# A prelude of attention and weight products: key sums by matmul, queries' shift on ScalarE, and a denser schedule

## The chip, the core and the metric

The kernel runs on one NeuronCore of a Trainium2 chip. The metric is the device time of one execution in microseconds, as the median of the runs shown. TensorE does matmuls and transposes, VectorE and ScalarE read its results out of PSUM, GpSimd works on SBUF, and DMA queues are fed by SyncE, ScalarE and GpSimd.

## The reference

Three layers follow one another over 2304 tokens (4 batches of 576). The kernel computes all of it in fp32 accuracy.

```python
def phi(x):                                   # per head, 64 -> 128 -> 256 features
    proj = x @ w_phi
    proj = proj - np.max(np.abs(proj), axis=-1, keepdims=True)
    return np.concatenate([np.exp(proj), np.exp(-proj)], axis=-1)
q_p, k_p = phi(q), phi(k)
kv = einsum('bhsf,bhsd->bhfd', k_p, v)
z  = sum(k_p, axis=2)                         # the key sums
attn = (q_p @ kv) / (q_p @ z + 1e-6)
x = ((attn @ w1) * (attn @ w2)) @ w3 @ w_out  # moe1
# moe2: route each token to one of 8 experts, relu(x @ ew1[e]) @ ew2[e], times the gate
```

## The kernel before

**Stages.** A first stage, the prelude, does two things at once. It folds `w3 @ w_out` into one matrix W (`build_w`, L216) and splits w1 and w2 into a high and a low fp32r part (`load_w12`, L199), and it works on attention for the first batch. Then moe1 runs over nine blocks of 256 tokens, each of eight `ab_unit`s (L596) and four products with W, with the rest of attention strewn between; then come the expert slots of moe2.

**W's units.** The weights come as 64-bit numbers, and `f64_to_f32` (L124) makes fp32 of each 512 KB tile by three integer operations on VectorE (L132, L134, L136); there are 8 tiles of w_out, 16 of w3 and 16 of w1 and w2. `wo_a` and `wo_b` (L235 on) convert and transpose w_out's chunks and multiply them with the expert embeddings, over a bank `pl` that four `wo_b` share. A `w_unit` (L275) is eight native fp32 matmuls, 16 records in the trace; there are 16 such units, two for each of eight column chunks, and each second one ends in splits of two banks `pw` into `wph` (ScalarE) and `wpl` (VectorE, L112).

**Attention's units.** The features of one head are two exponentials of a projection shifted by its largest magnitude. For keys, `phi_tile` (L307) projects a tile of 128 tokens and four heads into a PSUM bank `pphi`, VectorE takes the largest magnitude `mx` (L325), and `key_feats` makes eight activations on ScalarE (L339, L340). Then `kv` (L448) multiplies the features with v (`kv_native`, L394) into one bank that all pieces of a batch share. For z the features of all pieces are first added up on VectorE in `kacc` (L461), and `sums` (L468) multiplies the total with a block of ones, 32 columns wide, once for each of four heads (`key_sums`, L397). `fin` transposes both and splits them. For queries, `query_p` (L344) subtracts the largest magnitude from the projection on VectorE (L347) into `pt`; `tr` transposes one head of it (L539), and two activations (L542, L543) make the features `F`, which are split into `Hh` and `Ll`; `num` multiplies them with kv and z (bank `po`), and for each second head VectorE divides (`den`, L564, and `xf`, L568) and the result is split into moe1's input.

While `native` is set, projections are single fp32 matmuls (four records a tile) and the input tiles `qkraw` and `v` are requested from ScalarE's queue (`queue`, L367). Afterwards, the tile is split into `qkh` (ScalarE) and `qkl` (VectorE or GpSimd), the projection takes six fp32r matmuls, and requests go through SyncE's queue.

**What sets the order.** TensorE's instructions run in the order in which the program writes them (`manual_schedule(engines={PE})`, L1082 and L1106). The order on the other engines is made by the framework's scheduler when the kernel is built, and then fixed. Every unit of attention has a time in a planner's units: a key piece takes `KEY_T` 1.9, a head's query 1.04 + 0.65 times a quarter of its tiles; projections are put `LEAD_Q` 3.5 (queries) or `LEAD_K` 2.25 (keys) ahead, numerators `LEAD_N` 2.95 behind their transposes. `due[blk]` (L1072) is the time at which block blk of moe1 has its input; `due[0]` stands 1.5 behind the last numerator of the first chunk of 256 tokens. `attend(until)` (L1076) writes out all units whose time is below `until`. W's units cost 0.5 (`wo_a`, `wo_b` and the like, 18 of them) or 3.1 (`w_unit`, 16), 58.6 in total, and after each one the loop calls

```python
attend(START_T * (done / tot) ** START_P)     # START_T 32.0, START_P 0.7
```

so that at W's end all attention due before 32.0 is written. Then `native` is cleared, buffers for moe1 are made, `fill_scratch` writes fills to DRAM through SyncE's queue, and `attend(due[0])` writes what is left before moe1's first block.

**PSUM.** Three banks (`pm`) serve W, moe1 and routing, five (`pa`) all of attention, and in the prelude also `wo_a`, `wo_b` and `wo_c`.

Of the kernel before, what the change touches and what calls it, by code (L numbers as in the profile page):

```python
# [9 lines left out]
F32 = mybir.dt.float32  # L10
# [4 lines left out]
AF = mybir.ActivationFunctionType  # L15
# [8 lines left out]
NF = 128  # L24
# [3 lines left out]
P = 128  # L28
# [22 lines left out]
LEAD_Q = 3.5  # L51
LEAD_N = 2.95
GAP_K = 2.0
START_T = 32.0
START_P = 0.7
RAW64 = 3
PTB = 5
# [37 lines left out]
class Kern:  # L95
# [248 lines left out]
    def query_p(self, p3, m, keep):  # L344

        pt = self.ap.tile([P, 4, NF], F32, tag="ptk" if keep else "pt", name="pt", bufs=2 if keep else PTB)
        self.nc.vector.tensor_tensor(out=pt, in0=p3,  # L347
                                     in1=m.rearrange("p (h o) -> p h o", o=1).to_broadcast([P, 4, NF]),
                                     op=ALU.subtract)
        return pt  # L350
# [36 lines left out]
    def kv_native(self, kvp, v, kfs, r0, r1, first, last):  # L387
# [4 lines left out]
        for r in range(2):  # L392
            for c in range(2):
                self.nc.tensor.matmul(out(kvp, c * D, D, r * 256), lhsT=v[r0:r1, (2 * r + c) * D:(2 * r + c + 1) * D],  # L394
                                      rhs=kfs[r][r0:r1, :, c * NF:(c + 1) * NF],
                                      start=first and r == 0, stop=last and r == 1)
    def key_sums(self, zp, acc):  # L397

        for h in range(4):
            self.nc.tensor.matmul(zp[32 * h:32 * h + 32, 0:256].rearrange("p (s f) -> p s f", s=2), lhsT=self.one32,  # L400
                                  rhs=acc[h // 2][:, :, (h % 2) * NF:(h % 2 + 1) * NF], start=True, stop=True)

    def kv_split(self, b, pair, pv, pz):

# [14 lines left out]
    def key_units(self, out, time, b):  # L419

        nc = self.nc
        pieces = self.pieces(b)
        whole = int(pieces[0][1] > 0)
        for g in range(2):
            kvp = [None, None]
            acc = []
            for n, (t, r0, r1) in enumerate(pieces):
                st = {}

                def phi(st=st, t=t, n=n, g=g, r0=r0, r1=r1, whole=whole):  # L430
                    self.ph = int(b > 0)
                    st["v"] = self.load_v(t, g)
                    if r0:

                        st["f"] = self.kept[g]
                        return
                    keep = r1 < P

                    kind = ("kfk", 4) if keep else ("kacc", KACC) if n == whole else ("kf", KB_)
                    st["f"] = self.key_feats(*self.phi_tile("k", t, g), kind)  # L440
                    if keep:
                        self.kept[g] = st["f"]

                if not r0:
                    phi.raw = ("k", t, g)
                out.append((time - LEAD_K, phi))

                def kv(st=st, n=n, r0=r0, r1=r1, kvp=kvp, g=g, acc=acc):  # L448
                    if n == 0:
                        kvp[0] = self.app.tile([P, 512], F32, tag="pa", name="kv")  # L450
                    self.ph = int(b > 0)
                    last = n == len(pieces) - 1
                    self.kv_native(kvp[0], st["v"], st["f"], r0, r1, n == 0, last)
                    todo = [(st["f"], r0, r1)]
                    if n == whole:

                        todo = [(self.kept[g], *pieces[0][1:])] if whole else []
                        acc[:] = st["f"]
                    for f, a, e in todo if n >= whole else ():
                        for r in range(2):  # L460
                            nc.vector.tensor_tensor(out=acc[r][a:e], in0=acc[r][a:e], in1=f[r][a:e], op=ALU.add)  # L461
                    if last:

                        x = self.ap.tile([P, 512], F32, tag="pt", name="kvs0", bufs=PTB)
                        nc.scalar.copy(x, kvp[0])
                        kvp[0] = x

                def sums(kvp=kvp, acc=acc):  # L468
                    kz = self.app.tile([P, 512], F32, tag="pa", name="kz")
                    self.key_sums(kz, acc)  # L470
                    x = self.ap.tile([P, 320], F32, tag="xf", name="kvs1", bufs=1)
                    nc.scalar.copy(x[:, :256], kz[:, :256])
                    kvp[1] = x

                out.append((time + KV_D / 2, kv))
                time += KEY_T - 0.65 * (r0 > 0)

            def fin(kvp=kvp, g=g):
                self.ph = int(b > 0)
                ps = [self.app.tile([P, 512], F32, tag="pa", name=x) for x in ("pkv", "pkz")]  # L480
                for x, p, w in zip(kvp, ps, (512, 256)):
                    for a in range(0, w, P):
                        nc.tensor.transpose(p[:, a:a + P], x[:, a:a + P], self.ident)
                for r in range(2):
                    self.kv_split(b, 2 * g + r, *ps)

            out.append((time + SUM_K, sums))
            out.append((time + FIN_K, fin))
        return time + GAP_K
# [543 lines left out]
def tile_kernel(ctx, tc, qT, kT, vv, w_phi, w1, w2, w3t, w_out, emb, tau, ew1, ew2, out):  # L1033
    k = Kern(tc)
    nc = tc.nc
    maxrow = (NE - 1) * CAP + NT

    def pool(stack, name, side="left", **kw):
        return stack.enter_context(tc.tile_pool(name=name, bufs=kw.pop("bufs", 1), side=side, reuse_waits="tile", **kw))

    def regs(e, row, engines):
        return (nc.values_load(e, engines=engines, min_val=0, max_val=NE - 1),
                nc.values_load(row, engines=engines, min_val=0, max_val=maxrow))
# [28 lines left out]
    due = [ready[min(i for i, e in enumerate(chunk_end) if e >= (blk + 1) * BLK)] for blk in range(NBLK)]  # L1072
# [3 lines left out]
    def attend(until):  # L1076
        nonlocal ai
        while ai < len(attn) and attn[ai][0] < until:
            attn[ai][1]()
            ai += 1  # L1080

    with ExitStack() as c0, tc.manual_schedule(engines={PE}):  # L1082
        sp = pool(c0, "start")
        k.attn_init(apool, papool, sp, qT, kT, vv)
        k.attn_loads([u for _, u in attn])
        k.constants(cp, sp, w_phi)
        k.more_constants(cp, sp, pm, emb, tau)
        attend(START_0)
        lw = k.load_w12(sp, w1, w2, wt)
        wu = k.build_w(sp, pm, papool, w3t, w_out, wph, wpl)  # L1090

        tot = sum(c for c, _ in wu)
        done, n = 0.0, len(lw)
        for c, u in wu:
            u()
            done += c
            while lw and n - len(lw) < n * done / tot:
                lw.pop(0)()
            attend(START_T * (done / tot) ** START_P)
        k.native = False  # L1100
    mp = pool(c1, "moe1")
    for i in (1, 2):
# [2 lines left out]
    with ExitStack() as order:  # L1105
        order.enter_context(tc.manual_schedule(engines={PE}))  # L1106
        late = None
        for blk in range(NBLK):
            units, route, tail = k.moe1_units(blk, mp, pm, wt, wph, wpl, x2d, tab)
            attend(due[blk])  # L1110
            for i, (c, u) in enumerate(units):
                if i == 3 and late:
                    late()
                    late = None
                    if blk == EARLY:
# [5 lines left out]
                        e, row = regs(*k.early_slot(wa, pm), {SP})  # L1121
# [6 lines left out]
                n = (blk - EARLY) * len(units) + i - 3  # L1128
# [7 lines left out]
                else:  # L1136
                    b0 = EARLY - TAILB
                    f = ((blk - b0) * len(units) + i + 1) / (TAILB * len(units) + 3)
# [5 lines left out]
    with tc.manual_schedule(engines={ENG[x] for x in MENG}):  # L1144
# [6 lines left out]
        for s in range(NSTAT + 1):  # L1151
            loads = splits = ()
            for i, u in enumerate(cur[1] + cur[2]):
# [10 lines left out]
                if s < NSTAT and go:  # L1164
                    e, row = regs(k.ri[0:1, s:s + 1], k.ri[0:1, 4 + s:5 + s], {SP})
# [18 lines left out]
                if s == NSTAT and i == 2:  # L1184

                    cnt = nc.values_load(k.ri[0:1, 8:9], min_val=0, max_val=NLOOP)
                    e, row = regs(k.ri[0:1, 16:17], k.ri[0:1, 32:33], {SP})
# [7 lines left out]
    with tc.tile_pool(name="rest", bufs=1) as rp:  # L1195
        with tc.For_i(1, cnt, 1) as i:
            e, row = regs(k.ri[0:1, ds(i + 16, 1)], k.ri[0:1, ds(i + 32, 1)], {SP})
# [41 lines left out]
```

## Time and profile before

| | us |
|---|---|
| median of 3 runs | 867.17 (865.34 to 867.81) |
| the profiled execution's own time | 866.59 |
| its span, first to last instruction | 864.9 |
| TensorE busy in the span | 819.2 (95%) |
| VectorE | 536.9 (62%) |
| ScalarE | 402.9 (47%) |
| GpSimd | 240.4 (28%) |

The profile is of one execution. PE is TensorE's matmuls (PEld its weight loads), DVE VectorE, ACT ScalarE, POOL GpSimd, SP SyncE; a name with q is the engine's queue. A busy share is an average over stages with different limits, so the views below are asked for stretches of the span. A wait is the idle time of an engine just before an instruction, put down to what released it. One fp32 matmul is two records in the trace.

### The profile page before, as it was taken

What the parts mean: (1) busy time and instruction counts of PE and PEld (TensorE: products, weight loads), DVE (VectorE), ACT (ScalarE), POOL (GpSimd) and SP (SyncE); (2) the same over time, 40 slices, a digit from 0 to 9 for tenths busy, and PEclk for the clock granted to TensorE, in tenths of its full rate; (3) what the DMA queues carried; (4) which work ended last, traced back from release to release, by engine and by line L of the source; (5) the groups of instructions that cost most, each with busy time, mean ns of one, the idle gap of its engine ahead of it and who ended that gap; (6) DMA issues with size and microseconds to landing.
All of it is one profiled execution on the core that took longest, in us unless ns stands there. A gap on an engine that the chain in (4) does not pass through costs nothing. (4 is left out here: it accounts for less than half of the span.)

```text
span 864.9 us, 15449 instructions
## 1 busy us (share of the span) xinstructions
PE 819.2 (95%) x5730; PEld 734.5 (85%) x5730; DVE 536.9 (62%) x1226; ACT 402.9 (47%) x1105; POOL 240.4 (28%) x257
## 2 busy tenths in 40 slices
PE   6789978999999999999999999989999999999996
PEld 4467767998899987999888999989998898989974
DVE  6889996656779866797757794644375452432200
ACT  5454445455676557674555752213334342433211
POOL 2112353431255312463212642130013301211010
PEclk9999998899999999999999999989999999999998
DMA  6666642001211011210021000032207441622410
GB/s 205 223 202 201 198 125 76 26 22 60 57 24 50 13 56 52 55 45 19 26 67 44 25 14 1 26 105 80 91 26 248 161 147 43 194 87 86 158 41 15
DMA packets 63535, 73.43 MB, mean 85 GB/s; under 512 B 7832, under 2 KB 50072, under 8 KB 63458
## 3 DMA queue, kind: packets, MB, share of 16 engines
q1 hardware_dynamic: 53010, 58.88, 21.8%
q0 software_dynamic: 3680, 9.72, 3.3%
q10 hardware_dynamic: 6768, 3.82, 1.5%
q8 instruction: 46, 0.75, 0.4%
q14 instruction: 31, 0.25, 0.1%
HBM read 61.71 MB, written 10.95 MB: 84 GB/s over the span
## 5 line engine op out<-in xcount | busy, mean ns | idle before, releaser
L112 POOL TENSOR_TENSOR Ll<-F,Hh 128x512 fp32r<-128x512 f32 (+1 forms) x64 | 93.6, 1463 | 104.0 <-ACT Hh L104 95.7
L120 PE MATMUL px<-wph,abh 128*128 128x260 f32 x288 | 84.1, 292 | 4.9 <-DVE ab L609 3.5
L120 PE MATMUL pab<-xh,w1h 128*128 128x256 f32 x288 | 84.4, 293 | 0.1
L122 PE MATMUL px<-wph,abl 128*128 128x260 f32 x288 | 82.6, 287 | 0.0
L121 PE MATMUL px<-wpl,abh 128*128 128x260 f32 x288 | 82.5, 286 | 0.0
L121 PE MATMUL pab<-xl,w1h 128*128 128x256 f32 x288 | 81.8, 284 | 0.0
L122 PE MATMUL pab<-xh,w1l 128*128 128x256 f32 x288 | 81.8, 284 | 0.0
L120 PE MATMUL pab<-xh,w2h 128*128 128x256 f32 x288 | 81.5, 283 | 0.0
L121 PE MATMUL pab<-xl,w2h 128*128 128x256 f32 x288 | 81.5, 283 | 0.0
L122 PE MATMUL pab<-xh,w2l 128*128 128x256 f32 x288 | 81.4, 283 | 0.0
L120 PE MATMUL ph<-xsh,wth 128*128 128x256 f32 (+1 forms) x256 | 75.9, 296 | 0.6 <-ACT xsh L104 0.6
L121 PE MATMUL ph<-xsl,wth 128*128 128x256 f32 (+1 forms) x256 | 75.7, 296 | 0.5 <-DVE xsl L112 0.5
L122 PE MATMUL ph<-xsh,wtl 128*128 128x256 f32 (+1 forms) x256 | 75.6, 295 | 0.0
L285 PE MATMUL pw<-wo,y 128*128 128x260 f32 x256 | 64.6, 408 | 5.0 <-DVE wpl L112 3.3
L112 POOL TENSOR_TENSOR qkl<-qkraw,qkh 128x256 fp32r<-128x256 f32 x52 | 38.6, 745 | 110.5 <-ACT qkh L104 107.7
L607 ACT COPY a<-pab 128x256 f32<-128x256 f32 x72 | 27.2, 378 | 86.9 <-PE pab L122 71.2
L564 DVE RECIPROCAL den<-den 128x256 f32<-128x256 f32 (+1 forms) x32 | 62.3, 1947 | 7.8 <-ACT den L559 7.7
L943 DVE SCALAR_TENSOR_TENSOR hh<-ph,hh 128x256 fp32r<-128x256 f32 (+1 forms) x96 | 31.1, 353 | 57.9 <-ACT hh L939 51.0
L609 DVE TENSOR_TENSOR ab<-pab,a 128x256 f32<-128x256 f32 x72 | 30.4, 423 | 55.8 <-ACT a L607 55.4
L285 PEld LDWEIGHTS pw<-wo,y 128*128 128x128 f32 x256 | 50.8, 203 | 15.1 <-DVE wpl L112 4.9
L120 PEld LDWEIGHTS px<-wph,abh 128*128 128x128 f32 x288 | 55.6, 193 | 8.6 <-DVE ab L609 3.7
L325 DVE TENSOR_REDUCE mx<-pphi 128x4 f32<-128x512 f32 x72 | 49.2, 686 | 18.4 <-PE pphi L122 8.8
(230 smaller groups left out, 2408.9 us busy)
## 6 DMA issues: line engine op xcount, KB each, us to landing
wraw<-in_moe_w_dram SPq DMA_DIRECT2D x32, 512.0 KB
raw<-in_moe_w_dram SPq DMA_DIRECT2D x16, 512.0 KB
raw<-in_moe_w3t_dram SPq DMA_DIRECT2D x16, 512.0 KB
x2d<-x SPq DMA_DIRECT2D x18, 256.0 KB
raw<-in_moe_w_out_dram SPq DMA_DIRECT2D x8, 512.0 KB
pw<-in_moe_w_dram SPq DMA_DIRECT2D x8, 512.0 KB
v<-in_v_dram SPq DMA_DIRECT2D x30, 128.0 KB
qkraw<-in_qT_dram SPq DMA_DIRECT2D x27, 128.0 KB
```

The costliest lines, as they stand in the source:

```text
L112: e.tensor_tensor(out=out, in0=a, in1=b, op=ALU.subtract)
L120: nc.tensor.matmul(out, lhsT=lh, rhs=rh, start=start, stop=False)
L121: nc.tensor.matmul(out, lhsT=lh, rhs=rl, start=False, stop=False)
L122: nc.tensor.matmul(out, lhsT=ll, rhs=rh, start=False, stop=stop)
L285: nc.tensor.matmul(pss[u][:, :HB], lhsT=y[:, j, :], rhs=wo[:, jc, u, :], start=jc == 0, stop=jc == 7)
L325: nc.vector.tensor_reduce(out=m, in_=p3, axis=AX.X, op=ALU.max, apply_absolute_value=True)
L564: nc.vector.reciprocal(den[:, :n], den[:, :n])
L607: nc.scalar.copy(a, ps[:, :BLK])
L609: nc.vector.tensor_tensor(out=ab, in0=ps[:, BLK:], in1=a, op=ALU.mult)
L943: nc.vector.scalar_tensor_tensor(out=lo(h, i, j), in0=x, scalar=0.0, in1=h[:, i:j].bitcast(F32), op0=ALU.max, op1=ALU.subtract)
```

## The change

The key sums of the first batch are made by TensorE from each piece's features, accumulated in a bank of their own that is held from the first piece to the last; the additions on VectorE stay for the other batches only. While `native` is set, the queries' shift is made by a negation and four activations with a bias on ScalarE in place of one subtraction on VectorE. `START_T` goes: the attention written during W now runs up to `due[0]`, and reaches it at 1/1.04 of W's cost.

```diff
     def query_p(self, p3, m, keep):
         pt = self.ap.tile([P, 4, NF], F32, tag="ptk" if keep else "pt", name="pt", bufs=2 if keep else PTB)
+        if self.native:
+            mn = self.ap.tile([P, 4], F32, tag="mn", name="mn", bufs=4)
+            self.nc.scalar.mul(mn, m, -1.0)
+            for h in range(4):
+                self.nc.scalar.activation(out=pt[:, h, :], in_=p3[:, h, :], func=AF.Identity, bias=mn[:, h:h + 1])
+            return pt
...
-    def key_sums(self, zp, acc):
+    def key_sums(self, zp, kfs, r0=0, r1=P, first=True, last=True):
         for h in range(4):
-            self.nc.tensor.matmul(zp[32 * h:32 * h + 32, 0:256].rearrange("p (s f) -> p s f", s=2), lhsT=self.one32,
-                                  rhs=acc[h // 2][:, :, (h % 2) * NF:(h % 2 + 1) * NF], start=True, stop=True)
+            self.nc.tensor.matmul(zp[32 * h:32 * h + 32, 0:256].rearrange("p (s f) -> p s f", s=2),
+                                  lhsT=self.one32[r0:r1, :], rhs=kfs[h // 2][r0:r1, :, (h % 2) * NF:(h % 2 + 1) * NF],
+                                  start=first, stop=last)
...
                     if n == 0:
                         kvp[0] = self.app.tile([P, 512], F32, tag="pa", name="kv")
+                        if b == 0:
+                            kvp[1] = self.app.tile([P, 512], F32, tag="pa", name="kz")
...
                     self.kv_native(kvp[0], st["v"], st["f"], r0, r1, n == 0, last)
-                    todo = [(st["f"], r0, r1)]
+                    if b == 0:
+                        self.key_sums(kvp[1], st["f"], r0, r1, n == 0, last)
+                    todo = [(st["f"], r0, r1)] if b else []
...
-                    for f, a, e in todo if n >= whole else ():
+                    for f, a, e in todo if b and n >= whole else ():
...
                 def sums(kvp=kvp, acc=acc):
-                    kz = self.app.tile([P, 512], F32, tag="pa", name="kz")
-                    self.key_sums(kz, acc)
+                    if b:
+                        kvp[1] = self.app.tile([P, 512], F32, tag="pa", name="kz")
+                        self.key_sums(kvp[1], acc)
...
-            attend(START_T * (done / tot) ** START_P)
+            attend(due[0] * min(1.0, 1.04 * done / tot) ** START_P)
```

## Rows read from the trace of the kernel before

**Rows 1.** Busy time (records) by stretch, then TensorE's granted clock, DMA share, GB/s

```profile
0.00:154.50 154.50, 126.86 (x638) 96.80 (x639) 129.76 (x220) 72.29 (x208) 47.25 (x51) 0.92 0.55 173
44.00:130.00 86.00, 76.17 (x370) 59.77 (x369) 81.88 (x136) 37.56 (x113) 27.59 (x20) 0.96 0.59 181
130.00:154.50 24.50, 20.19 (x96) 17.42 (x97) 15.88 (x26) 12.66 (x29) 10.90 (x12) 0.78 0.21 73
154.50:200.00 45.50, 45.50 (x360) 43.81 (x361) 28.58 (x47) 24.32 (x68) 15.85 (x18) 0.97 0.10 30
200.00:700.00 500.00, 490.14 (x3837) 457.62 (x3834) 335.14 (x861) 260.19 (x733) 155.32 (x167) 0.99 0.20 60
```

The columns are stretch, its length, then PE, PEld, DVE, ACT and POOL.

**Rows 2.** TensorE's waits in the first 155 us: total us, times, longest

```profile
PE pt L242 <- DVE wo L136: 6.1, 4, 2.3
PE po L120 <- DVE xf L568: 5.3, 1, 5.3
...
PE pw L285 <- DVE wpl L112: 3.3, 2, 1.9
PE pw L285 <- DVE y L136: 1.7, 1, 1.7
PE pphi L122 <- DVE qkl L112: 1.3, 1, 1.3
PE po L121 <- POOL Ll L112: 1.3, 1, 1.3
PE pkz L483 <- ACT kvs L472: 1.2, 1, 1.2
PE pphi L120 <- ACT F L543: 1.1, 1, 1.1
```

**Rows 3.** TensorE's timeline: start, us, instruction, idle before it

```profile
94.87 3.30 PE L285 MATMUL pw<-wo,y 128*128 128x260 f32 x8 [1.92 <-DVE wpl L112]
...
132.13 5.79 PE L285 MATMUL pw<-wo,y 128*128 128x260 f32 x16
...
139.55 3.67 PE L285 MATMUL pw<-wo,y 128*128 128x260 f32 x16
...
150.08 0.58 PE L120 MATMUL pphi<-bd_h,qkh 128*128 128x256 f32 x1 [1.06 <-ACT F L543]
...
154.48 0.41 PE L120 MATMUL pab<-xh,w1h 128*128 128x256 f32 x1
```

**Rows 4.** TensorE's timeline at a split projection, first two of its six records

```profile
145.14 0.28 PE L120 MATMUL pphi<-bd_h,qkh 128*128 128x256 f32 x1
145.26 0.28 PE L121 MATMUL pphi<-bd_l,qkh 128*128 128x256 f32 x1
```

**Rows 5.** Timeline of a native key projection and its last activations

```profile
20.20 1.03 PE L315 MATMUL pphi<-bd,qkraw 128*128 128x256 f32 x4
...
23.93 0.37 ACT L339 ACTIVATE kf<-pphi,mx 128x128 f32<-128x128 f32 x1
24.18 0.38 ACT L340 ACTIVATE kf<-pphi,mn 128x128 f32<-128x128 f32 x1
```

**Rows 6.** VectorE's groups by line in the first 154.5 us: busy us, mean ns

```profile
L461 DVE TENSOR_TENSOR kacc<-kacc,kf 128x512 f32<-128x512 f32 x12 | 8.7, 728 | 0.0
...
L347 DVE TENSOR_TENSOR pt<-pphi,mx 128x512 f32<-128x512 f32 x9 | 6.0, 675 | 0.0
...
L461 DVE TENSOR_TENSOR kacc<-kacc,kfk 64x512 f32<-64x512 f32 x4 | 2.6, 676 | 0.0
```

**Rows 7.** TensorE's timeline at a group of key sums

```profile
85.89 0.64 PE L400 MATMUL kz<-kacc,one 128*32 128x256 f32 x8
86.46 0.66 PE L483 MATMUL pkv<-ident,kvs 128*128 128x128 f32 x4
```

**Rows 8.** ScalarE's waits in the first 155 us: total us, times, longest

```profile
ACT w2h L104 <- DVE y L136: 24.7, 8, 3.8
...
ACT kacc L339 <- PE kz L400: 5.1, 1, 5.1
```

More of the change, by code (lines that the diff above doesn't have):

```diff
@@ L53 @@
 GAP_K = 2.0
-START_T = 32.0
 START_P = 0.7
@@ L468, in sums @@
                 def sums(kvp=kvp, acc=acc):
-                    kz = self.app.tile([P, 512], F32, tag="pa", name="kz")
-                    self.key_sums(kz, acc)
+                    if b:
+                        kvp[1] = self.app.tile([P, 512], F32, tag="pa", name="kz")
+                        self.key_sums(kvp[1], acc)
                     x = self.ap.tile([P, 320], F32, tag="xf", name="kvs1", bufs=1)
-                    nc.scalar.copy(x[:, :256], kz[:, :256])
+                    nc.scalar.copy(x[:, :256], kvp[1][:, :256])
                     kvp[1] = x
```

## The prediction

> **What bounds the kernel now.** I read the busy time by stretch first. From 154.5 us on TensorE works 45.50 of 45.50 us, then 490.14 of 500: the rest of the kernel runs at TensorE's pace, so an earlier first matmul of moe1's first block should end the kernel earlier by as much. The first 154.5 us, the prelude, are another matter: TensorE works 126.9 us and idles 27.6. VectorE works 81.88 of 86 us in the middle stretch, so it is the fullest engine there, with TensorE, 76.17, not far behind [rows 1].
>
> Second, the list of TensorE's waits in the prelude says who made the gaps. Late VectorE work: 5.3 us for xf, 3.3 for wpl, 1.7 for y, together 10.3. The stretch between W's last matmul and moe1: 1.3 for qkl, 1.3 for Ll, 1.1 for F, together 3.7. The key stage: 1.2 for the copied key sums. The start: 6.1 for the w_out chunks [rows 2].
>
> Third, TensorE's timeline gives the clock behind those gaps. W's sixteen-record unit takes 3.67 us at 139.55, but 5.79 at 132.13, right behind the 5.3 us gap; the granted clock is 0.78 over 130 to 154.5, a mix of 2.4 GHz and, behind the gaps, 1.2 GHz. W's last matmuls run from 139.55, and moe1's first starts at 154.48: in between lie only eight units of attention [rows 1, 3].
>
> **The change part by part.**
>
> Schedule. The planner's numbers can be worked by hand: ten key pieces at 1.9 and a gap of 2 make 21.0, eight heads at 1.365 bring 31.92, and 2.95 + 1.5 give due[0] = 36.37. Before, W's loop emits units due before 32.0; eight (two numerators of the first chunk, one of the second, two transposes, three query projections) follow behind W. After, the last two calls reach 35.99 and 36.37, so all eight stand ahead of W's last unit, and attention runs up to 17% denser against W in program order (37.4 against 32 at the same share of W). What the change says, it does. The eight units' work doesn't vanish: it moves to where W's matmuls can cover its waits. The 3.7 us of tail waits go whole. So does the slow clock there: the records from 150.08 to 154.48 run at 1.2 GHz (some 12 of them 0.09 us longer each, 1.1), and the clock of 0.97 over the next 45.5 us is 1.4 more: 2.5 us [rows 1, 3]. The three moved projections turn native: four records in 1.03 us where six split ones take 0.28 + 5 x 0.12 = 0.88; +0.5 us of TensorE for the three [rows 4, 5]. They drop three casts on ScalarE and three qkl subtractions. Their next raw tiles are requested from ScalarE's queue instead of SP's: nothing on the path, and SP's queue, which there also carries the fills of x2d, loses three requests. If such a request held ScalarE up, the casts that free W's banks would be late; that is kept in the half below.
>
> Key sums. Sixteen additions leave VectorE, 8.7 + 2.6 = 11.3 us busy [rows 6]. TensorE gets 40 matmuls instead of 8: eight more groups of four heads. A group of eight records costs 0.57 us from its start to the next group's (85.89 to 86.46): the four heads overlap, since eight records one behind the other, at W's step of 0.22, would take 1.8 [rows 3, 7]. So +4.6 us. Bounds: 3.5 if two steps of 0.22 were all, 14 if nothing overlapped. I take the row, as it is the same instruction. The sums wait for the same features as kv, so no new wait stands in TensorE's queue; the W unit behind starts 0.57 later.
> The Trainium skill (TensorEngine Tiling (Array Packing), Tiling Modes, Key Properties) speaks against this part: changing the tiling mode drains TensorE, and behind a kv group in 64 columns the sums in 32 are one more change each. The row of kz has a mode change at both ends already [rows 7]; if each of the eight groups paid one more drain of 0.2 us, an estimate from that group's 0.64 us less two steps of 0.22, the gain below would be 1.6 us smaller.
> The bank for the sums is now held through a whole group, and kacc is free as soon as its piece's sums are made: the 5.1 us for which ScalarE waited for kz, with a pphi bank held behind it, go [rows 8].
>
> Queries. Ten subtractions of 0.68 us leave VectorE, 6.0 us busy for the nine in the prelude [rows 6]. ScalarE gets for each one negation and four activations; the like of them, the features, start 0.25 apart: 1.2 us each, 12 in all [rows 5]. ScalarE works 37.56 of 86 us in the middle [rows 1], so this hides; a query tile is ready 0.6 us later than by VectorE at best, and up to 3.8 later if a cast that waits for VectorE stands ahead of it [rows 8]. Projections lead their transposes by 3.5 planner units, over one W unit, so I cost it at nothing; without that lead, each of ten tiles would cost TensorE up to 3.8.
>
> **The sum.** VectorE works 129.8 us in the prelude; less 11.3 and 6.0 are 112.5: no longer the fullest. TensorE's 126.9 + 4.6 + 0.5 are. So the gain is what TensorE's gaps give back, less 5.1. On offer: 3.7 (tail), 1.2 (kz), 10.3 (late VectorE), and the clock: 1.4 behind the 1.92 us gap at 94.87 (3.30 against half of 3.67 for eight records) and 5.4 + 1.4 after 130 (0.22 of 24.5, 0.03 of 45.5), 8.2: together 23.4 [rows 1 to 3]. I take the tail, the key stage and the tail's clock whole (3.7 + 1.2 + 2.5 = 7.4), and half of late VectorE and of the other clock (5.2 + 2.9 = 8.1): VectorE is still 78% busy (112.5 of 144), in a fixed order, and 17% denser attention must be fitted in. 7.4 + 8.1 - 5.1 = 10.4 us. From the profiled execution's own 866.59 us that is 856.2; it stands 0.6 below the median of the runs, 867.17. Forecast: 856.8 us.
>
> Ends: all of it gives 23.4 - 5.1 = 18.3, 848.9 by the median, and some more if part of the 6.1 us for w_out also goes (half of the additions lie there): 845. None of it gives +5.1: 872.3.
>
> **The rivals.**
> 1. VectorE was the whole limit. Its 17.3 us are worth all their waits and no new one comes. For it: 95% busy in the middle. Against: TensorE is 89% busy there and can't yield more than its gaps [rows 1]. 845 to 850 us; chance 0.17.
> 2. TensorE is already full, and the gaps move rather than close: only the tail gives (3.7 + 2.5), the sums and projections take 5.1, and the median comes to 866.1. For it: those 89%. Against: 10.3 us of its waits name VectorE [rows 2]. 861 to 870 us; chance 0.15.
> 3. PSUM runs out in the key stage, slower. Five banks serve attention: kv, now also kz, and W's pl hold three, so two are left for projections and transposes. A projection's bank is held from 20.20 to the last activation's end at 24.56, 4.4 us [rows 5]. It decides if the two free banks are both under projections when a transpose of w_out comes: then each of five such projections up to W's first unit holds TensorE 4.4 us, 22 in all; less the 10.4 won that is 11.6 more than now, 878.8. Against: in the present trace no wait of TensorE names a bank of that stage [rows 2], though a pphi kept its own through the 5.1 us wait for kz [rows 8]. 870 to 880; chance 0.08.
>
> **How the numbers follow.** A measurement of this kernel tells about 0.3%, 2.6 us, from no change. The forecast's own case (850 to 861) has 0.60; all of it and rival 1 are faster; of rival 2 about a third lies below 864.6: faster 0.82. The rest of rival 2 is the same: 0.10. Rival 3 is slower: 0.08. The range of 8 in 10 runs from 846 to 865: it leaves out rival 3, the upper part of rival 2 and the bottom of rival 1.
>
> **What would show it.** Right: no xf or wpl wait of 2 us or more in TensorE's list, the 3.7 us of the tail gone, the first matmul of moe1 at about 144 directly behind W's last unit, VectorE near 112 us busy in the prelude and TensorE over 88% of it, a kz group still near 0.57 us. Wrong: a kz group near 1.8 us (no overlap), waits of TensorE for activations on pphi or pqt in the first 45 us (banks), ScalarE's negations behind casts with TensorE waiting for pt, or a first moe1 matmul that comes earlier without the end following it.

## The result, and the profile after

The changed kernel takes 854.60 us (median of 3, 853.71 to 854.96) against 867.17: a ratio of 0.9855, 95% interval 0.9833 to 0.9877, so 12.6 us faster. The forecast was 856.8, a gain of 10.4. The profiled execution took 854.60 of its own.

The span is 852.9 us, 12.0 less than before, and every engine's busy time but ScalarE's fell (TensorE 815.3, VectorE 518.6, ScalarE 411.5, GpSimd 238.9). That says little; the stretches say where. Busy time by stretch of the changed kernel, columns as in [rows 1]:

```profile
0.00:143.70 143.70, 125.10 (x696) 94.59 (x696) 112.73 (x191) 79.29 (x249) 44.05 (x47) 0.95 0.58 178
44.00:130.00 86.00, 79.31 (x414) 63.08 (x411) 72.75 (x124) 45.28 (x141) 30.57 (x24) 0.94 0.59 182
130.00:143.70 13.70, 12.60 (x66) 10.69 (x64) 9.55 (x14) 8.29 (x25) 6.94 (x5) 1.00 0.09 26
143.70:200.00 56.30, 56.16 (x449) 52.44 (x448) 35.07 (x71) 32.67 (x98) 19.06 (x25) 1.00 0.18 59
```

The 12.0 us come apart in three, against [rows 1]. TensorE's idle time in the prelude was 154.50 - 126.86 = 27.6 and is 143.70 - 125.10 = 18.6: 9.0. Its busy time fell by 1.8 although it has 58 records more (696 for 638). And the part behind the prelude went from 864.9 - 154.5 = 710.4 to 852.9 - 143.7 = 709.2: 1.2, with a granted clock of 1.00 to 200 us where it was 0.97. VectorE has 17.0 us less to do (129.76 to 112.73) and is no longer the fullest in the middle stretch: 72.75 of 86 us, TensorE 79.31.

TensorE's waits of 1 us or more in the first 155 us of the changed kernel (total us, times, longest):

```profile
PE pphi L314 <- DMA bd<-in_w_phi_dram: 5.2, 1, 5.2
PE po L119 <- DVE xf L580: 4.4, 1, 4.4
PE pt L265 <- ACT ls L256: 2.4, 1, 2.4
PE po L119 <- ACT pt L350: 2.3, 1, 2.3
PE pphi L314 <- ACT kf L339: 2.1, 1, 2.1
PE pphi L314 <- DVE xf L580: 1.0, 1, 1.0
```

Against [rows 2]: wo's 6.1, wpl's 3.3, y's 1.7, the 3.7 of the tail (qkl, Ll, F) and the 1.2 of the key sums are gone, 16.0 us. The 5.3 for xf became 4.4. New are 2.4 (ls, ScalarE's copy of w_out times the expert embeddings), 2.3 (pt, the queries' shift, now on ScalarE, which frees a bank), 2.1 (kf, a projection waiting for its bank) and 1.0: 7.8. So 16.0 of the 27.6 us of idle time closed, and 7.8 opened. (5.2 for the first weights by DMA stands in both kernels.)

TensorE's timeline of the changed kernel (start, us, instruction, idle before it) shows the tail, three of these gaps, and what stands behind one of them:

```profile
93.11 0.39 PE L119 MATMUL po<-Hh,ch 128*128 128x256 f32 x1 [2.32 <-ACT pt L350]
...
93.92 5.36 PE L284 MATMUL pw<-wo,y 128*128 128x260 f32 x16
...
114.56 0.39 PE L119 MATMUL po<-Hh,ch 128*128 128x256 f32 x1 [4.37 <-DVE xf L580]
...
138.54 1.99 PE L314 MATMUL pphi<-bd,qkraw 128*128 128x256 f32 x8 [1.04 <-DVE xf L580]
140.37 3.67 PE L284 MATMUL pw<-wo,y 128*128 128x260 f32 x16
143.68 0.47 PE L119 MATMUL pab<-xh,w1h 128*128 128x256 f32 x1
```

moe1 now begins right behind W's last unit, at 143.68 instead of 154.48 [rows 3]. The gap at 93 costs more than its 2.32: the W unit behind it takes 5.36 us where the one at full clock takes 3.67, so part of it ran at the 1.2 GHz level.

VectorE's timeline around the 4.4 us gap tells what kind of lateness is left:

```profile
106.60 0.43 DVE L111 TENSOR_TENSOR wpl<-pw,wph 128x260 fp32r<-128x260 f32 x1
108.60 0.43 DVE L131 TENSOR_SCALAR y<-raw 128x512 int32<-128x512 int32 x1 [1.57 <-POOL w2l L111]
109.06 1.64 DVE L133 SCALAR_TENSOR_TENSOR y<-raw,y 128x512 int32<-128x512 int32 x1
...
111.90 1.74 DVE L576 RECIPROCAL den<-den 128x256 f32<-128x256 f32 x1
113.56 0.62 DVE L324 TENSOR_REDUCE mx<-pphi 128x4 f32<-128x512 f32 x1
114.11 0.86 DVE L580 TENSOR_TENSOR xf<-po,den 64x256 f32<-64x256 f32 x2
```

and ScalarE's at the instruction that feeds the reciprocal:

```profile
108.73 0.47 ACT L571 ACTIVATE den<-po,eps 64x256 f32<-64x256 f32 x1
```

The denominators are ready at 109.20, but the reciprocal starts at 111.90: four instructions of the weights' conversion and split, from 109.06 on, stand ahead of it in the built order, one of them stretched to 1.64 us, and just before them VectorE had idled 1.57 us for GpSimd. The reciprocal is late by its place in the order.

What TensorE itself lacks in these gaps is a PSUM bank. No numerator reads xf or pt, and no projection reads kf or xf; these are the instructions that read a bank out last and so free it. Just before 114.56 all five banks of attention are in use: `po` of 99.25 and 103.70, `pphi` of 104.49 and 108.94, `pqt` of 109.80. Just before 93.11 they are too: two `pphi` from 84.23 on, `pqt` of 85.96 and 90.40, `po` of 89.50. So the rows for xf, pt and kf, 4.4 + 2.3 + 2.1 + 1.0 = 9.8 of the 18.6 us of idle time, are waits for a bank that a late VectorE or ScalarE has not yet emptied, and the 5.3 for xf before [rows 2] is of the same kind. This is read from the kernel and its trace; no run with another number of banks was made.

### The profile page after: what moved, and what is told of

It is laid out like the page before. It is cut to its first block, busy times and chain, and to the rows that moved or that the text cites. A ratio compares the mean times of both kernels' runs of the same rounds, so it can differ in the third digit from the quotient of the medians.

```text
span 852.9 us, 15584 instructions
## 1 busy us (share of the span) xinstructions
PE 815.3 (96%) x5788; PEld 730.1 (86%) x5788; DVE 518.6 (61%) x1197; ACT 411.5 (48%) x1152; POOL 238.9 (28%) x257
## 5 line engine op out<-in xcount | busy, mean ns | idle before, releaser
L119 PE MATMUL px<-wph,abh 128*128 128x260 f32 x288 | 83.5, 290 | 5.0 <-DVE abh L105 5.0
L119 PE MATMUL pab<-xh,w1h 128*128 128x256 f32 x288 | 84.2, 292 | 0.7 <-DVE ab L621 0.6
L121 PE MATMUL px<-wph,abl 128*128 128x260 f32 x288 | 82.0, 285 | 0.0
L120 PE MATMUL px<-wpl,abh 128*128 128x260 f32 x288 | 81.8, 284 | 0.0
L120 PE MATMUL pab<-xl,w2h 128*128 128x256 f32 x288 | 81.5, 283 | 0.0
L119 PE MATMUL pab<-xh,w2h 128*128 128x256 f32 x288 | 81.5, 283 | 0.0
L121 PE MATMUL pab<-xh,w2l 128*128 128x256 f32 x288 | 81.4, 283 | 0.0
L121 PE MATMUL pab<-xh,w1l 128*128 128x256 f32 x288 | 81.3, 282 | 0.0
L120 PE MATMUL pab<-xl,w1h 128*128 128x256 f32 x288 | 81.2, 282 | 0.0
L119 PE MATMUL ph<-xsh,wth 128*128 128x256 f32 (+1 forms) x256 | 75.9, 296 | 0.5 <-ACT xsh L103 0.5
L120 PE MATMUL ph<-xsl,wth 128*128 128x256 f32 (+1 forms) x256 | 75.8, 296 | 0.5 <-DVE xsl L111 0.5
L121 PE MATMUL ph<-xsh,wtl 128*128 128x256 f32 (+1 forms) x256 | 75.5, 295 | 0.0
L119 PEld LDWEIGHTS px<-wph,abh 128*128 128x128 f32 x288 | 54.8, 190 | 8.8 <-DVE abh L105 6.1
L284 PE MATMUL pw<-wo,y 128*128 128x260 f32 x256 | 61.9, 396 | 0.1
L883 POOL DMA_INDIRECT out_dram<-ob,ids x20 | 20.4, 1018 | 138.3 <-ACT ob L973 118.7
L111 DVE TENSOR_TENSOR wtl<-wraw,wth 128x512 fp32r<-128x512 f32 x64 | 41.2, 687 | 28.2 <-ACT wth L103 28.2
```

The lines of the kernel that those rows point to most:

```text
L111: e.tensor_tensor(out=out, in0=a, in1=b, op=ALU.subtract)
L119: nc.tensor.matmul(out, lhsT=lh, rhs=rh, start=start, stop=False)
L120: nc.tensor.matmul(out, lhsT=lh, rhs=rl, start=False, stop=False)
L121: nc.tensor.matmul(out, lhsT=ll, rhs=rh, start=False, stop=stop)
L284: nc.tensor.matmul(pss[u][:, :HB], lhsT=y[:, j, :], rhs=wo[:, jc, u, :], start=jc == 0, stop=jc == 7)
L883: self.nc.gpsimd.indirect_dma_start(out=out, out_offset=IndirectOffsetOnAxis(ap=ids[:m, i, 0:1], axis=0), in_=ob[:m, :], in_offset=None, b ...
```

## The experiments

Each part of the change can be switched off in the changed kernel. The line numbers of the experiments are the changed kernel's, whose L119 to L121, L284, L314 and L580 were L120 to L122, L285, L315 and L568 before.

```diff
  queries off
-        if self.native:
+        if False:
             mn = self.ap.tile([P, 4], F32, tag="mn", name="mn", bufs=4)
  sums off
-                        if b == 0:
+                        if False:
                             kvp[1] = self.app.tile([P, 512], F32, tag="pa", name="kz")
-                    if b == 0:
+                    if False:
                         self.key_sums(kvp[1], st["f"], r0, r1, n == 0, last)
-                    todo = [(st["f"], r0, r1)] if b else []
+                    todo = [(st["f"], r0, r1)]
-                    for f, a, e in todo if b and n >= whole else ():
+                    for f, a, e in todo if n >= whole else ():
-                    if b:
+                    if True:
  schedule off
-            attend(due[0] * min(1.0, 1.04 * done / tot) ** START_P)
+            attend(32.0 * (done / tot) ** START_P)
```

Times below are medians; each ratio is to runs of the kernel before made beside it, whose median was 866.5 to 866.7 in all three sets.

### One part alone

Sums alone has queries and schedule off:

> Key sums on TensorE alone; queries' shift and schedule as before. Theory (TensorE's gaps close, its new work is paid): VectorE loses 11.3 us of additions, which gives back some of the late-VectorE waits and the 1.2 us for kz, and costs 4.6 us of key sums: 861 to 866 us. Rival A (VectorE's time is the whole limit): all of the additions, 856. Rival B (only the schedule's tail gave anything): the cost alone, 872.

Measured: 858.24 us, ratio 0.9894 (0.9865 to 0.9924): 8.3 us faster.

Queries alone has sums and schedule off:

> The queries' shift on ScalarE alone; the seven native projections lose 4.8 us of VectorE. Theory: a part of that, 863 to 867 us. Rival A: all of it, 862. Rival B: 867.

Measured: 865.96, ratio 0.9992 (0.9974 to 1.0010): no difference that can be told.

Schedule alone has queries and sums off:

> The denser schedule alone; key sums and queries' shift on VectorE as before. Theory: the tail's 3.7 + 2.5 less 0.5 us, less what denser attention costs on a VectorE that is already 95% busy: 861 to 865 us. Rival A: VectorE has as much to do as before and W's end moves back by what it takes in: 867. Rival B: the whole gain, 855 to 857.

Measured: 859.45, ratio 0.9924 (0.9895 to 0.9953): 7.1 us faster. The first and the last came out better than the 861 at which the theory's ranges begin. Together the three make 8.3 + 0.6 + 7.1 = 16.0, against the 12.6 of the whole change; with the three intervals, near 4 us in the sum, that alone doesn't show a difference. TensorE's waits in the prelude of schedule alone:

```profile
PE pt L241 <- DVE wo L135: 6.9, 4, 3.6
PE pphi L314 <- DMA bd<-in_w_phi_dram: 5.7, 1, 5.7
PE pw L284 <- DVE y L135: 5.1, 6, 1.5
PE pt L265 <- ACT ls L256: 4.1, 1, 4.1
PE po L119 <- DVE xf L580: 3.8, 1, 3.8
```

The tail's waits are gone, but VectorE still makes wo and y late, 12.0 us against 6.1 + 1.7 [rows 2]. I put that down to the denser attention while additions and shift stay on VectorE; it is one profile, and the two were not told apart. In sums alone it is the other way round: the tail's waits stay (Ll 1.3 and F 1.1 in the list below), and wo has almost none.

```profile
PE po L119 <- DVE xf L580: 3.7, 1, 3.7
PE pw L284 <- DVE wpl L111: 2.1, 1, 2.1
...
PE po L120 <- POOL Ll L111: 1.3, 1, 1.3
PE pphi L119 <- ACT F L555: 1.1, 1, 1.1
...
PE pt L241 <- DVE wo L135: 0.9, 1, 0.9
```

### One part left out

Sums off:

> The change without its key sums: schedule and queries on ScalarE, additions on VectorE as before. Theory: tail and the shift's 6.8 us of VectorE, without the 4.6 us of sums: 857 to 863 us. Rival A: the shift's VectorE time alone, 860. Rival B: 851 to 855, the sums only cost.

Measured: 857.68, ratio 0.9892 (0.9866 to 0.9917).

Queries off:

> The change without the queries' part: the ten subtractions are on VectorE again. Theory: 855 to 859 us. Rival A: 6.8 us lost, 861. Rival B: no difference, 854.6.

Measured: 856.15, ratio 0.9858 (0.9828 to 0.9889).

Schedule off:

> The change with the schedule of before (32.0 at W's end): both pieces of VectorE's relief, the tail back. Theory: the tail's 6.2 us are lost, 858 to 863 us. Rival A: the schedule is neutral, 853 to 856. Rival B: nothing of the gain is left, 867 to 872.

Measured: 859.06, ratio 0.9902 (0.9876 to 0.9929). So with the other two parts in place the sums are worth 3.1 us, the schedule 4.5, and the queries 1.5, each as the difference to 854.6. The intervals of the first two touch that of the whole change only at their ends; that of the third holds its ratio, so no gain of the queries is shown by either way. All three came within the theory's ranges. The sums, worth 8.3 alone, are worth 3.1 beside the other two; by the ratios the difference is just clear of the intervals, so they and the rest close partly the same gaps.

### Does TensorE's new work cost what it takes?

The forecast charged 5.1 us for it, on the ground that TensorE is now the fullest engine. Here each group of key sums in the full change is made twice, the second time with a block of four columns that hold zeros, so that kz stays the same (`key_sums` gets the block as an argument, and the product is four rows high):

```diff
                         self.key_sums(kvp[1], st["f"], r0, r1, n == 0, False)
+                        self.key_sums(kvp[1], st["f"], r0, r1, False, last, self.run[:, 0, :].bitcast(F32))
```

> The changed kernel with each of its ten groups of key sums followed by a second one that adds zeros: 5.7 us more of TensorE in the prelude, nothing else. Theory (TensorE is now the fullest engine of the prelude): most of it shows, 858 to 860.5 us against the changed kernel's 854.6. Rival A (VectorE still sets the pace): the gaps take it, 855.

Measured: 854.58, ratio 0.9851 (0.9823 to 0.9880), the time of the changed kernel to 0.1 us; the theory's 858 to 860.5 lies outside the interval, which ends at 856.1. Busy time by stretch of this run, up to its first W unit, from there to moe1's first matmul, and both together:

```profile
0.00:44.30 44.30, 35.40 (x280) 21.62 (x281) 30.01 (x55) 26.08 (x84) 6.36 (x19) 1.00 0.68 219
44.30:143.67 99.37, 90.68 (x496) 73.36 (x496) 82.52 (x137) 54.01 (x165) 37.35 (x28) 0.97 0.52 161
0.00:143.67 143.67, 126.07 (x776) 94.98 (x776) 112.52 (x191) 80.08 (x249) 43.71 (x47) 0.98 0.57 179
```

The second stretch of the changed kernel, from its own first W unit to moe1:

```profile
46.18:143.68 97.50, 89.71 (x467) 73.31 (x464) 80.18 (x134) 53.03 (x165) 37.50 (x28) 0.96 0.52 161
```

And TensorE's timeline of this run at a doubled group:

```profile
21.92 0.64 PE L408 MATMUL kz<-kf,one 128*32 128x256 f32 x8
22.38 0.61 PE L408 MATMUL kz<-kf,run 128*4 128x256 f32 x8
22.93 0.66 PE L241 MATMUL pt<-ident,wo 128*128 128x128 f32 x4
```

Ten more groups, 80 records, at 0.57 us each would be 5.7 us. In the trace a doubled group takes 1.01 (21.92 to 22.93) where a single one took 0.57, so 0.44 more, an estimate of 4.4 in all. moe1 starts at 143.67, as in the changed kernel (143.68). TensorE's busy time is only 1.0 us more, with a granted clock of 0.98 instead of 0.95; its idle time is 1.0 us less. The clock over the whole span is 0.991 to 0.995 in all five runs, against 0.987 to 0.989 in the three of the changed kernel.

So the doubled work is free in the sum, but TensorE's waits took in only 1.0 us of it; the other 3.4 is met by records that ran faster. The stretches show where. Up to the first W unit, with six of the ten doubled groups, this run is 1.9 us shorter (44.30 against 46.18). From there to moe1, with the other four (1.8 us), it is 1.9 longer (99.37 against 97.50). That TensorE's capacity is not a limit in W's part is therefore not shown.

### Does VectorE's time have a price of its own?

The full change, with the sixteen additions on VectorE kept, though nothing reads their result:

```diff
-                    todo = [(st["f"], r0, r1)] if b else []
+                    todo = [(st["f"], r0, r1)]
-                    for f, a, e in todo if b and n >= whole else ():
+                    for f, a, e in todo if n >= whole else ():
```

> The changed kernel with the sixteen additions made on VectorE too, their result unused: 11.3 us more of VectorE in the prelude, TensorE's work the same. Theory: VectorE is at 124 of some 144 us again and late waits come back in part: 857 to 861 us. Rival A: all of it, 864 to 866. Rival B: none, 854.6.

Measured: 854.69, ratio 0.9866 (0.9834 to 0.9898). The theory's 857 to 861 was not borne out, though the interval reaches up to 857.8. The prelude of this run, and the largest of its waits:

```profile
0.00:143.13 143.13, 122.58 (x695) 92.39 (x696) 122.53 (x207) 79.74 (x249) 46.68 (x47) 0.98 0.57 179
```

```profile
PE pw L284 <- DVE wpl L111: 6.6, 3, 2.5
PE pphi L314 <- DMA bd<-in_w_phi_dram: 4.8, 1, 4.8
...
PE pt L241 <- DVE wo L135: 2.3, 1, 2.3
```

VectorE works 122.53 us, 9.8 more, and moe1 starts no later. TensorE idles 2.0 us more than in the changed kernel (143.13 - 122.58 = 20.6), and the granted clock, 0.98 for 0.95, makes up for it in this profile. The 4.4 for xf is gone, 6.6 for wpl and 2.3 for wo stand in its place: the built order changed, and other handovers became the late ones. I then made the same edit on sums alone, where queries and schedule are off:

> Schedule and queries as before; key sums on TensorE, and the sixteen additions made on VectorE too, their result unused. VectorE has as much to do as before, TensorE 4.6 us more; only the chain from the additions to the key sums is cut. If VectorE's time made the gain of the sums alone (858.2): back at 866 to 871 us. If cutting the chain made it (the key stage no longer waits for late additions, and the next group's features not for the sums): 857 to 860.

Measured: 864.09 (12 runs), ratio 0.9963 (0.9943 to 0.9983): 5.9 us slower than sums alone. That lies between its two forecasts. In that schedule the same VectorE work does cost. Its waits:

```profile
PE pphi L314 <- DMA bd<-in_w_phi_dram: 5.4, 1, 5.4
PE pt L241 <- DVE wo L135: 5.4, 3, 2.0
PE pw L284 <- DVE wpl L111: 3.4, 2, 2.3
PE pw L284 <- DVE y L135: 3.4, 3, 1.5
```

The waits for wo are back, 5.4 against 0.9. The last of this kind takes the additions out of the kernel before and puts nothing in their place, so that the first batch's key sums are those of one tile alone:

```diff
-                    for f, a, e in todo if n >= whole else ():
+                    for f, a, e in todo if b and n >= whole else ():
```

> The kernel before without the sixteen additions, so that the first batch's z is that of its first tile alone: VectorE loses 11.3 us, TensorE gains nothing to do, and the sums don't wait for the last piece. If VectorE's time made the gain: 850 to 856 us, the sums' own cost not paid. If TensorE's cost is hidden as the doubled sums showed: the same as with the sums alone, 857 to 860.

Measured: 860.50, ratio 0.9926 (0.9905 to 0.9947): 6.0 us faster than the kernel before, and not faster than sums alone, which makes all the sums on TensorE. That is 0.5 above the upper of its two forecasts, which had TensorE's cost hidden. So of the 8.3 us of sums alone 5.9 come with taking the additions out. The other 2.4, by which the run with sums and additions both is still faster than before, I put down to the shorter chain behind the last piece, where the sums no longer wait for an addition; that was not tested by itself. The 6.0 here holds that shorter chain too, and not TensorE's new work, so it does not confirm the 5.9 by itself. The additions also keep a piece's features in their buffers longer, and taking them out changes the built order; neither was told apart from their time on VectorE.

### Is the attention's pace well chosen?

The exponent `START_P` sets how early in W attention is written; 0.7 is the changed kernel's.

```diff
-START_P = 0.7
+START_P = 0.6
```

> The changed kernel with the exponent 0.6 in place of 0.7: more of the attention in W's first part, where TensorE works 35 of 46 us. If the first part still has room: 851 to 854 us. If it is bound by its chains, W starts later and nothing is won: 855 to 858.

Measured: 854.73, ratio 0.9862 (0.9838 to 0.9886). And with 0.85:

> The changed kernel with the exponent 0.85: W starts earlier, attention is denser at its end. If the later part's handovers set the end: 857 to 862 us. If W's start does: 851 to 854.

Measured: 856.87, ratio 0.9881 (0.9854 to 0.9907). Neither is told from the changed kernel, and neither reached the 851 to 854 of a better pace. W's last unit starts at 141.14 in the late one, not before 140.37, and it now has a wait of 1.42 us for the queries' transfer just ahead of it. No version tried beats the changed kernel.

## Why the prediction was right, and where it was not

**The frame held.** The prelude was where time could be won, since right behind it TensorE has no gaps (56.16 of 56.30 us to 200): moe1's start moved by 10.8 us and the end by 12.0. The other 1.2 fits the clock behind moe1's start (1.4 forecast). moe1 was forecast at about 144 and came at 143.68, VectorE's work at 112.5 and came at 112.73. The schedule does what the planner's sums said: W's last unit is the last thing ahead of moe1, and the tail's 3.7 us are gone whole.

**The sum, by the three heads of the first section.** Idle time was to fall by 3.7 + 1.2 + 5.2 = 10.1; it fell by 9.0. Busy time was to rise by 5.1 of new work less 1.1 and 2.9 of clock, 1.1; it fell by 1.8. The rest was to give 1.4 and gave 1.2. So the forecast was 1.6 us of span too small, and busy time is why: it was 2.9 better than forecast.

**The step that was mis-sized: "half of the other clock".** Of the prelude's 6.8 us on offer (1.4 behind the gap at 94.87, 5.4 after 130) I took 4.0: 1.1 in the tail whole, and half of the rest. The clock from 130 us to moe1 is 1.00, where it was 0.78 over the old stretch [rows 1], so the 5.4 came whole, though it counts the clock over 4.3 us of idle time too (24.50 - 20.19) and is an upper bound. The 1.4 did not: another gap of 2.3 stands at 93, with 5.36 us of W behind it. That makes 1.4 of the 2.9; the other 1.5 I can't place in the rows. An estimate from the granted clocks of the two preludes puts it into the new work: the clock gave back 0.08 of 154.5 less 0.05 of 143.7, 5.2 us, and as busy time fell by 1.8, some 3.4 us of work were added and not 5.1.

**The step that doubling did not bear out: "less 5.1", because TensorE is the fullest engine.** The size of the groups was right. Key sums take as long as the old group did, in the timeline of the changed kernel:

```profile
15.83 0.64 PE L405 MATMUL kz<-kf,one 128*32 128x256 f32 x8
16.28 1.04 PE L252 MATMUL pl<-woT,enT 128*8 128x128 f32 x8
...
24.46 0.64 PE L405 MATMUL kz<-kf,one 128*32 128x256 f32 x8
25.03 0.66 PE L241 MATMUL pt<-ident,wo 128*128 128x128 f32 x4
```

0.45 and 0.57 from start to next start, the heads overlapping. By the Trainium skill (TensorEngine Tiling (Array Packing), Tiling Modes, Key Properties) a change of the tiling mode drains TensorE. These groups have one at each end, but the trace shows no price for it beyond the row of before, and no room for another 0.2 us of drain. Yet doubling the groups left the time where it was. The forecast charged new work at a fixed clock; in the doubled run the clock was higher, and that met most of the work, while the waits took in 1.0 us. What the groups cost in the changed kernel itself was not measured apart. TensorE was 87% busy (125.10 of 143.70), just under the 88 I had named.

**"Half of late VectorE" was right in size and doubtful in reason.** 10.3 us became 5.4 (4.4 and 1.0 for xf), so one sign named, no xf wait of 2 us or more, did not come. That VectorE is still 78% busy is not shown to be the cause: with 9.8 us more work on it no longer time can be told. The wpl and y waits went, and the xf wait that stayed is one of order, for a bank. Waits that I had no term for nearly cancelled each other: 6.1 for wo went, 2.4 + 2.3 + 2.1 came. That the sum came so near is in part luck.

**"I cost it at nothing" of the queries' shift** was too good at one place: TensorE waited 2.3 us once for pt, though the lead over the transposes was there. It did not need the shifted queries themselves; the numerators at 93.11 needed the bank that the shift reads out. ScalarE's negation for it stood behind a cast that waits for VectorE, a sign of wrong that I had named, and VectorE's mx for it was ready no earlier (at 91.37, the cast done at 91.43):

```profile
90.69 0.68 DVE L324 TENSOR_REDUCE mx<-pphi 128x4 f32<-128x512 f32 x1
90.81 0.62 ACT L103 CAST w2h<-y 128x512 fp32r<-128x512 f32 x1 [4.74 <-PE pqt L551]
91.41 0.21 ACT L348 ACTIVATE mn<-mx 128x4 f32<-128x4 f32 x1
...
91.91 1.14 ACT L350 ACTIVATE pt<-pphi,mn 128x128 f32<-128x128 f32 x4 [0.30 <-ACT mn L348]
```

ScalarE's two groups of the shift over the whole prelude:

```profile
L350 ACT ACTIVATE pt<-pphi,mn 128x128 f32<-128x128 f32 x40 | 11.7, 377 | 0.9 <-PE pw L284 0.5 <-ACT mn L348 0.3
L348 ACT ACTIVATE mn<-mx 128x4 f32<-128x4 f32 x10 | 2.1, 208 | 9.4 <-DVE mx L324 9.4
```

These are up to 145 us, by line: 11.7 + 2.1 us of work for the 12 of the forecast, but 9.4 us of idling for mx. The step no longer runs on VectorE, and still waits for it. Moving it gave no gain that the runs can tell.

**The rivals.** VectorE as the whole limit (845 to 850) fell: its 17 us less did not close its waits. TensorE already full (861 to 870) fell by the time itself, 854.60, and by the 9.0 us of idle time that closed. PSUM running out did not make the kernel slower, but it is there in small: a projection waits 2.1 us in the first 45 us for the bank that kf's activation frees, a sign that I had named, and the waits for xf and pt are for banks too, 9.8 us in all. I had read xf's as late VectorE work alone. Neither fewer nor more banks for attention were tried, so how near the kernel is to that limit stays open.

**What limits the prelude now** is, as far as the trace tells, single handovers in orders fixed at build time, half of the idle time by way of the five banks; the xf and pt cases above are read from the trace. Which of the other orders makes which wait was not settled, nor what more banks would give.

## What to carry to other kernels

Before a new instruction is charged to the fullest engine, look at what its idle time is made of, and test the charge by adding the work twice; then look stretch by stretch at what took it in, since a time that stays the same can be work in the gaps or a higher clock. Ask of each wait what is lacking: a result, or the bank that its releaser frees. Parts of a change that close the same gaps don't add up (the sums gave 8.3 us alone, 3.1 beside the rest), and a resource can have a price under one schedule (5.9 us for VectorE's additions) and none that can be told under another (0.1 us), so measure a part in the kernel where it will stand. A gap also costs what the clock takes behind it: here the W unit behind one took 5.36 us for 3.67, and with the last gaps ahead of moe1 gone the clock behind its start was 1.00 where it was 0.97.

## What was not expected of the hardware

More TensorE work went with a higher granted clock: 0.991 to 0.995 over the span in the five runs with doubled sums, 0.987 to 0.989 in the three without, and 1.00 against 0.93 in the stretch up to the first W unit, in the one profile of each. So 47 records more in that stretch took no more busy time, 35.40 us against the 35.37 of this row of the changed kernel:

```profile
0.00:46.18 46.18, 35.37 (x233) 21.27 (x233) 32.55 (x58) 26.25 (x85) 6.54 (x19) 0.93 0.70 213
```

That the added records raised the clock, and not a changed order around them, isn't shown.
